# Attention with feature products feeding a gated unit: another plan for the order of the work, an fp32 down projection in the first slots, phi from PSUM, and later kv sums

## The chip, the cores and the metric

The kernel runs on one core of a Trainium2 chip. A core has engines that work side by side, each through its own instructions in order: TensorE (PE in the profile, its weight loads PEld), VectorE (DVE), ScalarE (ACT), GpSimd (POOL) and SyncE (SP), from whose queue all transfers here are issued. The metric is the device time of one execution in microseconds (us). Matmuls write to PSUM, everything else lives in SBUF; one tensor, called the scratch, lies in DRAM.

## The reference

A linear attention without softmax, and behind it a gated feed-forward layer. For 4 batches, 4 heads, 1088 positions and head size 32:

```
phi(x)[i*8+j] = (S1 x)[i] * (S2 x)[j]          # 8 x 8 = 64 features per head
kv  = sum over s of phi(k_s) v_s^T              # 64 x 32, per batch and head
z   = sum over s of phi(k_s)                    # 64
x   = phi(q) kv / (phi(q) z + 1e-6)             # 4352 rows of 128 (heads side by side)
xn  = x / sqrt(mean(x^2) + 1e-6) * rms_g
out = (silu(xn w_gate) * (xn w_val)) w_out      # 128 -> 1536 -> 128
```

Everything is float32. S1, S2 and the three weight matrices come as 64-bit words and are turned into float32 on VectorE (with one step that ScalarE can take).

## The kernel before, in words

**Chunks and slots.** The 4352 rows are cut into eight chunks of 512 and one of 256 columns. The 1536 hidden units are cut into twelve blocks j of 128. One *slot* is one chunk with one block: two products (gate into `g_ps`, value into `v_ps`, L682), a Silu on ScalarE (L689), the product `h` on VectorE (L693, one operand from PSUM, one from SBUF), and the down projection into `o_ps` (L713). Each of these products is made of three passes in a reduced-precision format, since each operand is split into a high and a low half: `h_hi` is a cast (L210, mostly ScalarE), `h_lo` the difference (L218 on VectorE or L217 on GpSimd). There are 108 slots. The first 24 run as blocks 0 to 5 for chunk 0, 0 to 5 for chunk 1, then 6 to 11 for each; later chunks run all twelve blocks. The last two slots (`EXACT`) take the down projection in one fp32 matmul (L700) with `w_end`, the sum of the two weight halves made on GpSimd (L748).

**Weights.** `weights(j)` loads one block of all three matrices (128 x 384 words), converts it in five steps on VectorE (L265 or, on ScalarE, L289; L269, L274, L279, L283), casts the high half (L210) and subtracts for the low half (L217/L218), each as one instruction over 384 columns.

**The kv side** (`kside`). For each batch: products with S1 and S2 (L425) into PSUM, a copy to SBUF by ScalarE (L440), the outer product phi (L431, GpSimd; for batch 0 VectorE may take it), then the sums. For batches 0 and 1 the matmuls of L459 sum kv and z at once. For batches in `TURNED` (2 and 3) the matmuls of L356 sum the transposed kv, GpSimd adds phi over the positions (`zsum`, four adds, L364), and a transpose (L378) and small matmuls (L383) bring both into place.

**The query side** (`qside`). Chunks 0 and 1 make phi in row layout: products (L492), a copy (L515), the outer product `phn` (L499, GpSimd or VectorE), transposes (L509), a copy (L527). Later chunks write the products (L538, L542) to the scratch (`far`, L544) and load them back repeated, two `at` (L548) and four `bt` (L555) loads for a chunk, and multiply (L561, GpSimd or VectorE). Then comes the numerator and denominator in one set of matmuls (L580), the division (L598, L599, L590), the mean square and its root (GpSimd, L625), scaling (L628), a transpose (L632) and the halves `x_hi` (L647) and `x_lo` (L635).

**What sets the order.** Every operation is a task with an estimated duration on each engine that may take it, a key, and the tiles that it reads and writes. `Plan.run` walks through an estimated time with one clock for an engine; among the tasks that are ready it takes the one with the smallest key. A slot's key is its number; side work has keys some slots before its due slot. Buffers of one name are taken in the order in which the tasks were added. The result fixes the order of each engine's instructions and of the transfers in SP's queue; on the chip an instruction starts when its data are there, and nothing else ties the engines together.

Of the kernel before, what the change touches and what calls it, by code (L numbers as in the profile page):

```python
# [20 lines left out]
R = 8  # L21
F = R * R
# [16 lines left out]
RAWS, WBUFS, TBUFS = 7, 3, 2  # L39
ACCUM = 2  # L40
MEAN = 0
LOOK = 350
# [3 lines left out]
PHI_DVE = 300  # L46
# [7 lines left out]
URGENT = -45  # L54
# [4 lines left out]
ABS_ACT = 150  # L59
# [5 lines left out]
TURNED = (2, 3)  # L65
HBUFS = 3
GAIN = -28.5
EXACT = 2
HEAD = 2
K1 = (14, 16, 18, -9)  # L70
K1O = ()
KVO = ()
Q0 = (-58, -50, -50)
Q0L = -97.8
Q1 = (9, 7, 6)
Q1L = -20
KO = -12
# [22 lines left out]
class Plan:  # L100
# [11 lines left out]
    def add(self, ways, key, reads=(), writes=()):  # L112
        deps = {self.writer[x] for x in reads}
# [35 lines left out]
    def run(self, clock, filler, slow, urgent, window):  # L149
        clock, todo, out = dict(clock), self.tasks, []  # L150
        while todo:
            found = {e: [] for e in clock}
            for t in todo[:window]:
                r = self.ready(t)
                if r is None:
                    continue
                e = min(t.ways, key=lambda e: max(clock[e], r) + t.ways[e][0] + t.ways[e][2])
                found[e].append((r, t))
# [5 lines left out]
            ns, emit, _ = t.ways[e]  # L164
# [13 lines left out]
def attention_then_glu(ctx, tc, kT, v, qT, sw, w, gain, out):  # L178
# [16 lines left out]
    def act(n, key, emit, reads, writes, sbuf=False):  # L195
        plan.add({"act": (n * 0.835 + (92 if sbuf else 51), emit, 0)}, key, reads, writes)

    def dve(ns, key, emit, reads, writes):
        plan.add({"dve": (ns + 68, emit, 0)}, key, reads, writes)
# [7 lines left out]
    def copy(n, key, out, in_, reads, writes, penalty=COPY_DVE):  # L207

        plan.add({
            "act": (n * 0.835 + 92, lambda: nc.scalar.copy(out=out(), in_=in_()), 0),  # L210
            "dve": (n * 0.52 + 68, lambda: nc.vector.tensor_copy(out=out(), in_=in_()), penalty),
        }, key, reads, writes)

    def rest(n, key, out, in_, hi, reads, writes, penalty=REST_DVE):
# [3 lines left out]
            "dve": (n * 1.04 + 68, lambda: nc.vector.tensor_tensor(out=out(), in0=in_(), in1=hi(), op=ALU.subtract), penalty),  # L218
# [26 lines left out]
    w_end = const.tile([P, max(EXACT, 1), P], F32, name="w_end")  # L245
# [13 lines left out]
    def to_f32(n, key, dst, raw, tmp, reads, tt, writes, side=None):  # L259
# [30 lines left out]

        plan.add({"dve": (n * 0.52 + 68, a, 0), "act": (n * 0.835 + 92, a_act, ABS_ACT)}, key, reads, tt)
        dve(n * 0.52, key, b, tt, tt)
        if side:
# [19 lines left out]
            dve(n * 0.52, key - 1, top, reads, apart)  # L313
            dve(n * 1.04, key - 1, low, [*reads, *apart], apart)
            dve(n * 0.52, key, shift, tt, tt)
            dve(n * 1.04, key, join, [*tt, *apart], writes)
            return
        dve(n * 0.52, key, c, tt, tt)
        dve(n * 1.04, key, e, (*reads, *tt), tt)
        dve(n * 1.04, key, f, (*reads, *tt), writes)  # L320
# [10 lines left out]

    def weights(j, key, early):
        raw = sb("w_raw", [P, 3 * P, 2], RAWS, U32)
        f, tmp = sb("w", [P, 3 * P], WBUFS), sb("w_tmp", [P, 3 * P], TBUFS)
# [6 lines left out]
        to_f32(3 * P, key, f, raw, tmp, [raw], [tmp], [f])  # L341
        hi, lo = (x[:, j].rearrange("p a n -> p (a n)") for x in (w_hi, w_lo))
        copy(3 * P, key, lambda: hi, f, [f], [("w_hi", j)])
        rest(3 * P, key, lambda: lo, f, lambda: hi.bitcast(F32), [f, ("w_hi", j)], [("w_lo", j)])
# [54 lines left out]
    def kside(b, keys, early):  # L399
# [15 lines left out]
        for i, (lo, hi) in enumerate(groups):  # L415
# [13 lines left out]
            def outer(eng, ab=ab, phi=phi, ts=ts, m=m):  # L429
                a = ab()[:, ts].rearrange("p t h c r -> p (t h) c r")  # L430
# [8 lines left out]
            act(
                HALF * m, kab, lambda ab=ab, ab_ps=ab_ps, ts=ts, m=m: nc.scalar.copy(  # L440
                    out=ab()[:, ts].rearrange("p t h c r -> p (t h) c r"),
                    in_=ab_ps()[:, :m * HALF].rearrange("p (th c r) -> p th c r", c=2, r=R),
                ), [ab_ps], [(ab, i)],
            )
# [30 lines left out]
    def qside(c, keys, early):  # L475
# [6 lines left out]
        if c < NATURAL:  # L482

            ab, pn = sb("abq", [P, 4, H, 2, R], 1), sb("phn", [P, 4, H * F], 1)
            for u in range(0, nt, 2):
                us = slice(u, u + 2)
# [326 lines left out]
```

## Time and profile before

| | |
|---|---|
| median of three runs | 300.51 us (296.71 to 304.61) |
| the profiled execution | 299.74 us |
| its span, from the first to the last instruction | 297.9 us |
| granted TensorE clock, mean | 0.971 |
| busy: PE, DVE, ACT, POOL | 275.7, 206.1, 157.2, 88.5 us |

The profile is one execution, seen by the hardware profiler. Busy times add the instructions of an engine; matmuls are pipelined and their ends are modelled, so that a busy TensorE need not be at its peak. "Idle before, releaser" tells how long an engine stood idle ahead of an instruction and what ended that. The chain of waits is followed back from the last instruction, at each step to what released it. The granted clock is the share of full speed that TensorE was given.

### The profile page before, as it was taken

How to read it: one execution, taken by the hardware profiler on the slowest of the kernel's cores; microseconds unless marked ns; L12 is line 12 of the kernel's file. 1: busy time of each engine (PE TensorE's matmuls, PEld its weight loads, DVE VectorE, ACT ScalarE, POOL GpSimd, SP SyncE). 2: the span in 40 equal slices, each digit the busy share in tenths (PEclk: the TensorE clock that was granted, in tenths of full speed). 3: DMA queues.
4: the chain of work that ended last, by engine and by line, in shares of the span. 5: the costliest groups of instructions: out<-in, count | busy, mean ns of one | idle time of the engine just before them, and what ended most of it. 6: DMA issues, size and time to landing. Idle time of an engine off the chain costs nothing.

```text
span 297.9 us, 4938 instructions
## 1 busy us (share of the span) xinstructions
PE 275.7 (93%) x1832; PEld 215.4 (72%) x1832; DVE 206.1 (69%) x370; ACT 157.2 (53%) x316; POOL 88.5 (30%) x82
## 2 busy tenths in 40 slices
PE   7886995897979999899699999999999999999995
PEld 5765773665757767678578677877786888788895
DVE  3799899997558656574765577468656966677531
ACT  4454563545535644365356366546645755565562
POOL 3165655447233392330310211103010302100062
PEclk9997796899999999999899999999999999999999
DMA  6975822000420005114104200411050102100000
GB/s 204 380 274 176 261 67 84 2 0 2 132 61 35 2 31 155 47 34 137 62 2 140 54 35 5 136 38 37 18 139 3 37 11 68 37 1 0 2 35 19
DMA packets 12680, 22.09 MB, mean 74 GB/s; under 512 B 1584, under 2 KB 5616, under 8 KB 12656
## 3 DMA queue, kind: packets, MB, share of 16 engines
q1 hardware_dynamic: 12656, 21.78, 23.2%
q8 instruction: 14, 0.23, 0.3%
q14 instruction: 10, 0.08, 0.1%
HBM read 18.69 MB, written 3.08 MB: 73 GB/s over the span
## 4 chain that ended last, share of the span: by engine, by line
PE 55%; DVE 14%; DMA 13%; SPq 5%; issue 4%; ACT 4%; POOL 4%; DVEq 0%; POOLq 0%; ACTq 0%
PE g_ps L682 16%; PE v_ps L682 15%; PE o_ps L713 15%; DMA bt<-far 8%; DMA far<-abt 3%; SPq L555 3%; PE att L580 3%; DVE h L693 3%; DVE w_tmp L279 2%; DVE w_tmp L269 2%; DVE h_lo L218 2%; SPq L548 2%; ACT h_hi L210 2%; DMA q<-qT 2%; PE att L538 1%
## 5 line engine op out<-in xcount | busy, mean ns | idle before, releaser
L210 ACT CAST h_hi<-h 128x512 fp32r<-128x512 f32 (+1 forms) x106 | 63.5, 600 | 89.0 <-DVE h L693 85.8
L218 DVE TENSOR_TENSOR h_lo<-h,h_hi 128x512 fp32r<-128x512 f32 x76 | 57.5, 757 | 40.0 <-ACT h_hi L210 39.6
L693 DVE TENSOR_TENSOR h<-v_ps,s 128x512 f32<-128x512 f32 (+2 forms) x109 | 70.9, 652 | 19.3 <-PE v_ps L682 11.6
L217 POOL TENSOR_TENSOR h_lo<-h,h_hi 128x512 fp32r<-128x512 f32 (+1 forms) x30 | 34.4, 1151 | 123.6 <-ACT h_hi L210 123.5
L689 ACT ACTIVATE s<-g_ps 128x512 f32<-128x512 f32 (+1 forms) x108 | 61.6, 571 | 11.3 <-PE g_ps L682 10.3
L682 PE MATMUL g_ps<-x_hi,w_hi 128*128 128x512 f32 (+2 forms) x111 | 45.8, 412 | 0.0
L682 PE MATMUL g_ps<-x_hi,w_lo 128*128 128x512 f32 (+2 forms) x111 | 42.6, 384 | 2.6 <-DVE w_lo L218 2.6
L682 PE MATMUL v_ps<-x_hi,w_hi 128*128 128x512 f32 (+2 forms) x111 | 43.7, 394 | 0.9 <-DVE h L693 0.9
L713 PE MATMUL o_ps<-h_lo,w_hi 128*128 128x512 f32 (+1 forms) x106 | 41.9, 395 | 2.0 <-POOL h_lo L217 1.0
L682 PE MATMUL g_ps<-x_lo,w_hi 128*128 128x512 f32 (+2 forms) x111 | 42.6, 384 | 0.0
L713 PE MATMUL o_ps<-h_hi,w_hi 128*128 128x512 f32 (+1 forms) x106 | 42.5, 401 | 0.0
L682 PE MATMUL v_ps<-x_hi,w_lo 128*128 128x512 f32 (+2 forms) x111 | 42.3, 381 | 0.0
L682 PE MATMUL v_ps<-x_lo,w_hi 128*128 128x512 f32 (+2 forms) x111 | 42.2, 380 | 0.0
L713 PE MATMUL o_ps<-h_hi,w_lo 128*128 128x512 f32 (+1 forms) x106 | 41.2, 389 | 0.0
L713 PEld LDWEIGHTS o_ps<-h_lo,w_hi 128*128 128x128 f32 x106 | 20.2, 191 | 9.2 <-DVE h_lo L218 3.1
L682 PEld LDWEIGHTS g_ps<-x_hi,w_lo 128*128 128x128 f32 x111 | 21.4, 192 | 7.5 <-DVE w_lo L218 2.9
L682 PEld LDWEIGHTS v_ps<-x_hi,w_hi 128*128 128x128 f32 x111 | 21.3, 192 | 6.4 <-DVE h L693 2.2
L682 PEld LDWEIGHTS g_ps<-x_hi,w_hi 128*128 128x128 f32 x111 | 21.2, 191 | 5.4 <-issue 1.0
L682 PEld LDWEIGHTS g_ps<-x_lo,w_hi 128*128 128x128 f32 x111 | 21.3, 192 | 4.5 <-DVE x_lo L635 0.2
L682 PEld LDWEIGHTS v_ps<-x_lo,w_hi 128*128 128x128 f32 x111 | 21.2, 191 | 4.3
L682 PEld LDWEIGHTS v_ps<-x_hi,w_lo 128*128 128x128 f32 x111 | 21.2, 191 | 4.0 <-issue 0.2
L713 PEld LDWEIGHTS o_ps<-h_hi,w_hi 128*128 128x128 f32 x106 | 20.1, 190 | 4.9 <-issue 0.4
(99 smaller groups left out, 307.4 us busy)
## 6 DMA issues: line engine op xcount, KB each, us to landing
w_raw<-w SPq DMA_DIRECT2D x12, 384.0 KB
at<-far SPq DMA_DIRECT2D x12, 256.0 KB
bt<-far SPq DMA_DIRECT2D x24, 128.0 KB
vt<-v SPq DMA_DIRECT2D x12, 204.0 KB
kt<-kT SPq DMA_DIRECT2D x12, 192.0 KB
q<-qT SPq DMA_DIRECT2D x8, 256.0 KB
outT<-o_sb SPq DMA_DIRECT2D x8, 256.0 KB
far<-abt SPq DMA_DIRECT2D x6, 128.0 KB
```

Source lines behind the costliest of these rows:

```text
L210: "act": (n * 0.835 + 92, lambda: nc.scalar.copy(out=out(), in_=in_()), 0),
L217: "pool": (n * 2.1 + 150, lambda: nc.gpsimd.tensor_tensor(out=out(), in0=in_(), in1=hi(), op=ALU.subtract), 0),
L218: "dve": (n * 1.04 + 68, lambda: nc.vector.tensor_tensor(out=out(), in0=in_(), in1=hi(), op=ALU.subtract), penalty),
L269: nc.vector.tensor_scalar(out=t, in0=t, scalar1=LEAST, scalar2=MOST, op0=ALU.max, op1=ALU.min)
L279: nc.vector.scalar_tensor_tensor(out=u, in0=r[:, :, 1], scalar=0xC0000000, in1=u, op0=ALU.bitwise_and, op1=ALU.bitwise_or)
L548: P * n * 4, kab, lambda p=p, rows=rows: nc.sync.dma_start(out=at()[:, p, :n], in_=far()[rows, :n].unsqueeze(1).to_broadcast([2 * R, R, n] ...
L555: F * n * 4, kab, lambda p=p, o=o, rows=rows: nc.sync.dma_start(out=bt()[o * F:(o + 1) * F, p, :n], in_=far()[rows, :n].unsqueeze(0).to_br ...
L580: nc.tensor.matmul(out=nv[hf * HALF:(hf + 1) * HALF, t, p, :], lhsT=phi()[:, p, l0:l0 + HALF], rhs=kvs[(s0 + l0) // S][:, p, :], start=Tru ...
L682: nc.tensor.matmul(out=acc()[:, cs], lhsT=wt[:, j, i3, :], rhs=x()[:, cs], start=(i == 0), stop=(i == 2))
L689: act(n, t + 0.3, lambda: nc.scalar.activation(out=s()[:, :n], in_=gps()[:, :n], func=AF.Silu), cols(gps, whole[0]), [s])
L693: lambda cs=cs: nc.vector.tensor_tensor(out=h()[:, cs], in0=vps()[:, cs], in1=s()[:, cs], op=ALU.mult),
L713: nc.tensor.matmul(out=o_ps()[:, :n], lhsT=wt[:, j, 2, :], rhs=x()[:, :n], start=first and i == 0, stop=last and i == 2,)
```

## The change

1. **The plan.** Each way of doing a task now carries a mark whether it uses the SBUF port that VectorE and GpSimd share (all of GpSimd's, and VectorE's with SBUF operands alone). `run` keeps one more clock, `port`: a marked task starts after the last marked one has ended, and where the other engine has a marked task with a smaller key, due before this one would end, that goes first. Fixed costs are raised (ScalarE 92 and 51 to 172 and 144 ns, VectorE 68 to 140), phi on GpSimd costs 530 ns a tile in place of 477, a step to a task of an engine that could take both costs 30 ns. The loads from the scratch count twice their bytes. `LOOK` goes from 350 to 150, `URGENT` from -45 to -1, `ABS_ACT` from 150 to -300.
2. **The first twelve slots** (`EARLY`) take the down projection as one fp32 matmul from `h` and `w_f`, the converted weights, which now stay in SBUF whole; `w_end` and its two GpSimd adds go. The high and low halves of the weights are made in two pieces, gate and value (256 columns) with the conversion, and w_out (128 columns) by tasks with keys from 6 to 16.
3. **Phi from PSUM.** For batch 0 (all groups but one), batch 1 and chunks 0 and 1 of the queries VectorE makes phi with the first factor straight from PSUM; ScalarE copies only the second factor. What is not made so goes to GpSimd.
4. **The kv side.** Batch 1 is turned as well. Batches 2 and 3, whose keys stood 12 slots before chunks 2 and 3, now stand 20, 18 and 16 slots before the chunks that first need them, 4 and 6. Batch 1's keys go from 14, 16, 18 to 8, 9, 10, and its tasks are added behind chunk 1's.
5. **Chunk 0's second half** of the query side has keys 20 later than the first.

The core of the diff:

```diff
-LOOK = 350
+LOOK = 150
-URGENT = -45
+URGENT = -1
-ABS_ACT = 150
+ABS_ACT = -300
-TURNED = (2, 3)
+TURNED = (1, 2, 3)
+EARLY = 12
+SPLIT = 6
-K1 = (14, 16, 18, -9)
+K1 = (8, 9, 10, -9)
-KO = -12
+KO = (20, 18, 16)
...
-            at = max(at, self.ready(t))
+            o = {"dve": "pool", "pool": "dve"}.get(e)
+            if o and t.ways[e][3]:
+                due = max(at, self.ready(t), port) + t.ways[e][0]
+                rivals = [x for r, x in found[o] if x.ways[o][3] and x.key < t.key and max(r, clock[o]) < due]
+                if rivals:
+                    e, t = o, min(rivals, key=lambda t: t.key)
+                    at = clock[o]
+            at = max(at, self.ready(t), port if t.ways[e][3] else 0)
...
+            if shared:
+                port = clock[e]
...
+    def split(j, xs, key):
+        n = (xs.stop - xs.start) * P
+        f, hi, lo = (x[:, j, xs].rearrange("p a n -> p (a n)") for x in (w_f, w_hi, w_lo))
+        ids = [(j, x) for x in range(xs.start, xs.stop)]
+        copy(n, key, lambda: hi, lambda: f, [("w", j)], [("w_hi", *y) for y in ids])
+        rest(n, key, lambda: lo, lambda: f, lambda: hi.bitcast(F32), [("w", j)] + [("w_hi", *y) for y in ids], [("w_lo", *y) for y in ids])
...
-        copy(3 * P, key, lambda: hi, f, [f], [("w_hi", j)])
-        rest(3 * P, key, lambda: lo, f, lambda: hi.bitcast(F32), [f, ("w_hi", j)], [("w_lo", j)])
+        split(j, slice(0, 2), key)
...
-            ways = {"pool": (m * 477, lambda outer=outer: outer(nc.gpsimd), 0)}
-            if first:
-                ways["dve"] = (m * 268 + 68, lambda outer=outer: outer(nc.vector), PHI_DVE)
-            plan.add(ways, kphi, [(ab, i)], [(phi, i)])
+            if near:
+                dve(m * 268, kphi, lambda outer=outer: outer(nc.vector), [(ab, i), ab_ps], [(phi, i)])
+            else:
+                pool(m * 530, kphi, lambda outer=outer: outer(nc.gpsimd), [(ab, i)], [(phi, i)])
...
-                    P * n * 4, kab, lambda p=p, rows=rows: nc.sync.dma_start(
+                    P * n * 8, kab, lambda p=p, rows=rows: nc.sync.dma_start(
...
-        if left < EXACT:
+        if left < EXACT or t < EARLY:
...
-                        out=o_ps()[:, cs], lhsT=w_end[:, left], rhs=h()[:, cs], start=first, stop=last and cs.stop == n
+                        out=o_ps()[:, cs], lhsT=w_f[:, j, 2], rhs=h()[:, cs], start=first, stop=last and cs.stop == n
...
-    kside(1, K1[:3], K1[3])
+    for j in range(NJ):
+        split(j, slice(2, 3), max(EARLY, slots.index((0, j))) + j % CUT - SPLIT if (0, j) in slots else 0)
     t1 = begin[1]
     qside(1, [t1 - x for x in Q1], Q1L)
+    kside(1, K1[:3], K1[3])
     for t, (c, j) in enumerate(slots):
         slot(c, j, t)
         if j == (CUT - 1 if c == 0 else NJ - 1):
-            if c + 2 < B:
-                kside(c + 2, [begin[min(len(begin) - 1, c + 2)] + KO] * 3, begin[c + 1] - 5)
             if c + 2 < len(CHUNKS):
                 t2 = begin[c + 2]
+                if c in (2, 4):
+                    kside(c // 2 + 1, [t2 - x for x in KO], t2 - KO[0] - 5)
                 qside(c + 2, [t2 - x for x in QO], t2 - 20)
```

More of the change, by code (lines that the diff above doesn't have):

```diff
@@ L149, in run @@
     def run(self, clock, filler, slow, urgent, window):
-        clock, todo, out = dict(clock), self.tasks, []
+        clock, todo, out, port = dict(clock), self.tasks, [], 0
         while todo:
@@ L195, in act, with dve @@
     def act(n, key, emit, reads, writes, sbuf=False):
-        plan.add({"act": (n * 0.835 + (92 if sbuf else 51), emit, 0)}, key, reads, writes)
-    def dve(ns, key, emit, reads, writes):
-        plan.add({"dve": (ns + 68, emit, 0)}, key, reads, writes)
+        plan.add({"act": (n * 0.835 + (172 if sbuf else 144), emit, 0)}, key, reads, writes)
+    def dve(ns, key, emit, reads, writes, shared=False):
+        plan.add({"dve": (ns + 140, emit, 0, shared)}, key, reads, writes)
     def pool(ns, key, emit, reads, writes):
@@ L289, in a_act @@
             nc.scalar.activation(out=t, in_=r[:, :, 1].bitcast(F32), func=AF.Abs)
-        plan.add({"dve": (n * 0.52 + 68, a, 0), "act": (n * 0.835 + 92, a_act, ABS_ACT)}, key, reads, tt)
-        dve(n * 0.52, key, b, tt, tt)
+        plan.add({"dve": (n * 0.52 + 140, a, 0, True), "act": (n * 0.835 + 172, a_act, ABS_ACT)}, key, reads, tt)
+        dve(n * 0.52, key, b, tt, tt, True)
         if side:
@@ L311, in join @@
                 )
[L313 to L316, printed above, removed]
+            dve(n * 0.52, key - 1, top, reads, apart, True)
+            dve(n * 1.04, key - 1, low, [*reads, *apart], apart, True)
+            dve(n * 0.52, key, shift, tt, tt, True)
+            dve(n * 1.04, key, join, [*tt, *apart], writes, True)
             return
-        dve(n * 0.52, key, c, tt, tt)
-        dve(n * 1.04, key, e, (*reads, *tt), tt)
-        dve(n * 1.04, key, f, (*reads, *tt), writes)
+        dve(n * 0.52, key, c, tt, tt, True)
+        dve(n * 1.04, key, e, (*reads, *tt), tt, True)
+        dve(n * 1.04, key, f, (*reads, *tt), writes, True)
     load(P * NB * 8, -99, lambda: nc.sync.dma_start(out=s_raw.rearrange("p n c -> p (n c)"), in_=sw.bitcast(U32)), ["s_raw"])
@@ L427, in mm, with outer @@
                         )
-            def outer(eng, ab=ab, phi=phi, ts=ts, m=m):
-                a = ab()[:, ts].rearrange("p t h c r -> p (t h) c r")
+            near = i not in FAR if first else b in NEAR
+            def outer(eng, ab=ab, phi=phi, ts=ts, m=m, near=near, ab_ps=ab_ps):
+                both = ab()[:, ts].rearrange("p t h c r -> p (t h) c r")
+                a = ab_ps()[:, :m * HALF].rearrange("p (th c r) -> p th c r", c=2, r=R) if near else both
                 eng.tensor_tensor(
@@ L482, in qside @@
         if c < NATURAL:
-            ab, pn = sb("abq", [P, 4, H, 2, R], 1), sb("phn", [P, 4, H * F], 1)
+            ab, pn = sb("abq", [P, 4, H, R], 1), sb("phn", [P, 4, H * F], 1)
             for u in range(0, nt, 2):
+                kab = keys[0] + (LATER if first and u else 0)
                 us = slice(u, u + 2)
@@ L571, in qside @@
         for u in range(0, nt, 2):
+            knum = keys[1] + (LATER if first and u else 0)
             num, den, rden, sq = ps("att", 3), sb("den", [P, 8, 1], 2), sb("rden", [P, 8, 1], 2), sb("sq", [P, 2, DM], 2)
@@ L612, in qside @@
                 267, knum, lambda u=u, sq=sq: nc.vector.tensor_reduce(out=ss()[:, u:u + 2], in_=sq(), axis=AX.X, op=ALU.add),
-                [sq], [(ss, u), (ss, u + 1)],
+                [sq], [(ss, u), (ss, u + 1)], True,
             )
         for u, wd in ((0, 2), (2, 2)) if first else ((0, nt),):
+            kturn = keys[2] + (LATER if first and u else 0)
             us, cs = slice(u, u + wd), slice(u * P, (u + wd) * P)
@@ L716, in down @@
                     )
-            pe(n * 1.36, t + 2.5, down, [h_hi, h_lo, ("w_hi", j), ("w_lo", j)], cols(o_ps, whole[0]))
+            pe(n * 1.36, t + 2.5, down, [h_hi, h_lo, ("w_hi", j, 2), ("w_lo", j, 2)], cols(o_ps, whole[0]))
         if not last:
```

94 lines of the change are left out of this document (43 added, 51 removed).

## The prediction

> **What bounds the kernel now.** I read the page first, then a cut of the span into stages, the chain of waits, the groups of instructions, and last the instructions in order of time where these pointed. On the page TensorE is busy nearly always and the chain is mostly TensorE; that is an average over stages that differ, so the cut comes next (columns: length of the stretch, busy time of each engine with its count, granted clock, DMA).
>
> ```profile
> PE 275.7 (93%) x1832; PEld 215.4 (72%) x1832; DVE 206.1 (69%) x370; ACT 157.2 (53%) x316; POOL 88.5 (30%) x82
> ```
> ```profile
> 20.00:66.00 46.00, 39.38 (x290) 29.42 (x288) 44.95 (x74) 23.16 (x54) 26.04 (x18) 0.85 0.35 112
> 66.00:85.00 19.00, 16.98 (x152) 12.60 (x151) 13.20 (x19) 10.30 (x20) 7.89 (x8) 1.00 0.28 73
> 85.00:169.00 84.00, 77.38 (x502) 59.06 (x500) 52.21 (x92) 41.52 (x75) 27.81 (x21) 0.98 0.21 63
> 169.00:293.00 124.00, 123.41 (x672) 99.99 (x673) 82.46 (x150) 72.15 (x139) 20.30 (x22) 1.00 0.12 36
> ```
>
> From 169 to 293 us TensorE is busy 123.4 of 124 us: nothing but fewer matmuls can shorten that stage. From 20 to 66 us VectorE is busy 44.95 of 46 us and the granted clock is down to 0.85: VectorE is the bound there. From 85 to 169 us TensorE lacks 6.6 us. The gain has to come from the front and the middle.
>
> Why VectorE is full in front is seen in single instructions (start, duration, engine).
>
> ```profile
> 28.04 0.35 DVE L269 TENSOR_SCALAR w_tmp<-w_tmp 128x384 f32<-128x384 f32 x1
> 28.31 0.55 DVE L279 SCALAR_TENSOR_TENSOR w_tmp<-w_raw,w_tmp 128x384 uint32<-128x384 uint32 x1
> 28.78 0.35 DVE L274 TENSOR_SCALAR w_tmp<-w_tmp 128x384 uint32<-128x384 uint32 x1
> 29.05 0.55 DVE L283 SCALAR_TENSOR_TENSOR w<-w_raw,w_tmp 128x384 uint32<-128x384 uint32 x1
> ...
> 21.87 1.66 DVE L274 TENSOR_SCALAR w_tmp<-w_tmp 128x384 uint32<-128x384 uint32 x1
> 23.72 1.85 DVE L279 SCALAR_TENSOR_TENSOR w_tmp<-w_raw,w_tmp 128x384 uint32<-128x384 uint32 x1
> ...
> 104.44 0.69 DVE L693 TENSOR_TENSOR h<-v_ps,s 128x512 f32<-128x512 f32 x1 [1.19 <-PE v_ps L682]
> ```
> ```profile
> 21.51 1.81 POOL L431 TENSOR_TENSOR phi<-ab 128x768 f32<-128x768 f32 x1 [0.71 <-ACT ab L440]
> 23.60 1.56 POOL L431 TENSOR_TENSOR phi<-ab 128x768 f32<-128x768 f32 x1 [0.28 <-ACT ab L440]
> ...
> 102.67 5.35 POOL L431 TENSOR_TENSOR phi<-ab 128x768 f32<-128x768 f32 x3
> ```
>
> The steps of a weight conversion take 0.35 and 0.55 us; the two that start just after a GpSimd phi take 1.66 and 1.85 and end when it has ended. The h product at 104.44, which reads PSUM and one SBUF tile, takes its usual 0.69 in the middle of GpSimd's phis. So SBUF work of the two engines excludes each other, and an operand from PSUM escapes it. The groups give the bill.
>
> ```profile
> L279 DVE SCALAR_TENSOR_TENSOR w_tmp<-w_raw,w_tmp 128x384 uint32<-128x384 uint32 x12 | 11.0, 916 | 0.0
> L283 DVE SCALAR_TENSOR_TENSOR w<-w_raw,w_tmp 128x384 uint32<-128x384 uint32 x12 | 9.8, 814 | 0.0
> L269 DVE TENSOR_SCALAR w_tmp<-w_tmp 128x384 f32<-128x384 f32 x12 | 7.6, 637 | 0.0
> L274 DVE TENSOR_SCALAR w_tmp<-w_tmp 128x384 uint32<-128x384 uint32 x12 | 6.6, 550 | 0.1
> L431 POOL TENSOR_TENSOR phi<-ab 128x768 f32<-128x768 f32 x10 | 18.1, 1817 | 7.9 <-ACT ab L440 7.9
> L431 DVE TENSOR_TENSOR phi<-ab 128x768 f32<-128x768 f32 x1 | 1.0, 959 | 0.0
> L217 POOL TENSOR_TENSOR h_lo<-h,h_hi 128x512 fp32r<-128x512 f32 x20 | 27.1, 1358 | 100.4 <-ACT h_hi L210 100.3
> L364 POOL TENSOR_TENSOR zsum<-phi 128x768 f32<-128x768 f32 x2 | 3.7, 1836 | 0.1
> ```
>
> Against 0.55 and 0.35 us, the four conversion steps lose 12 x (0.37 + 0.26 + 0.29 + 0.20) = 13.4 us to waiting, nearly all of it between 20 and 66 us. VectorE's own work there is then 45 - 13 = 32 us, beside 26 us of GpSimd.
>
> **The change, part by part. The front.** Of GpSimd's 26.0 us go: the three phi of batch 1 (to VectorE, from PSUM), 3 x 1.8 = 5.5; two phi and a first zsum add of batch 2 (later), 5.5; about seven h_lo, as the twelve first slots go down whole in fp32, 7 x 1.36 = 9.5; one query phi, 1. That is 21.5. New there: batch 1 is turned now and has zsum adds, two of 1.84 and two shorter ones, 5.5 us in all by an estimate of half length for the short; and the low halves of the weights, now in two pieces a weight (24 instead of 12, the second pieces around slots 6 to 16). Where these land is the plan's choice: none on GpSimd or all of them, 0 to about 13 us (twelve of 0.75 and twelve of 0.35, scaled from the phi rate by length); I take 4. GpSimd keeps 4.5 + 5.5 + 4 = 14 us, and with waiting in proportion VectorE loses 13 x 14/26 = 7 us instead of 13. Bounds: 2 us, if its adds fall beside the products from PSUM, to 13, if they don't.
>
> VectorE's own work stays about equal: three h_lo less and the mask step moved to ScalarE for most weights (about -3), against three phi of 0.96 and one more query phi (+3.8). Its new phi reads one operand from PSUM; the h product shows that as neither slower nor blocked. ScalarE has room: 23.2 of 46 us busy, with twelve h_hi casts gone and some conversions and twelve short copies added. Up to the end of the weights VectorE has 32 + 7 = 39 us in place of 45; counted on to 85 us it has 32 + 11 of its own (the 13.2 of the second row less some 2 of waiting) and 7 + 2 of waiting: 52 us where the stretch was 65 us long.
>
> TensorE's floor for the same slots, from the chain of waits in order of time (start, duration, what):
>
> ```profile
> 26.84 0.84 PE att L425 x12
> 27.68 1.23 PE att L459 x24
> 28.91 1.05 PE att L492 x4
> 36.35 0.71 PE g_ps L682 x3
> 67.66 0.81 PE att L356 x48
> 73.89 0.88 PE att L538 x2
> 75.39 2.58 DMA far<-abt
> 81.21 5.10 DMA bt<-far
> ```
>
> A slot is three such triples, 2.1 us; 17 of them to 85 us are 35.7. Beside them lie the 72 phi matmuls of batches 1 and 2 at 0.07 us (5.0), batch 1's 72 L459 (3.7), batch 2's 72 L356 (1.2), L538 (0.9) and about 5 of chunk 1's query side and the turning (an estimate from the 1.05 row): 51 us of 65. The change takes out batch 2 (36 L425, 72 L356 and its turning, 4 us in all, which come back later) and makes batch 1's 72 L459 into 72 L356 plus a turning (-2). The fp32 down is bounded by the L538 row, one fp32 matmul over 512 columns: 0.88 against 0.71, so twelve slots cost +2 us, and most of it lies under VectorE's bound. Floor: 51 - 4 - 2 + 2 = 47 us, below VectorE's 52. Add 2 for gaps between the two, and slot 17 stands at 20 + 54 = 74 instead of 85. With batch 2's 4 us repaid in a stage that TensorE bounds, the front is worth 11 - 4 = 7 us, from 0 (waits not reduced) to 14 (TensorE's floor).
>
> By the page on the gate ("TensorE: Matmul & The Clock Gate", What's actually happening) of the Trainium skill the clock halves after an idle window of about 3.4 us. Were the 0.85 of the front to stay, 47/0.85 = 55 us would be that floor, and the front would be worth 6. No run here shows yet whether the clock recovers when VectorE is relieved.
>
> **The middle.** TensorE's own waits between 85 and 169 us, and the clock after the longest:
>
> ```profile
> 87.84 1.04 PE L580 MATMUL att<-kv,phiq 128*64 128x66 f32 x28 [1.69 <-POOL phiq L561]
> 123.69 1.04 PE L580 MATMUL att<-kv,phiq 128*64 128x66 f32 x28 [1.42 <-DVE phiq L561]
> 145.13 1.04 PE L580 MATMUL att<-kv,phiq 128*64 128x66 f32 x28 [2.30 <-POOL phiq L561]
> 146.10 0.67 PE L713 MATMUL o_ps<-h_hi,w_hi 128*128 128x512 f32 x1
> 149.86 0.39 PE L713 MATMUL o_ps<-h_hi,w_hi 128*128 128x512 f32 x1
> ```
>
> All three are the numerator's matmuls, put into TensorE's order before phi is there. Phi waits for the scratch: 2.58 us for the store and, from its end at 77.97 to the end of the last load at 86.31, 8.3 us for six loads. The old plan believes in 0.77 us for an `at` load, 0.39 (raised to its least step of 0.5) for a `bt`, and 1.9 after the last: 5.4 us. The new doubles the loads: 2 x 1.54 + 4 x 0.77 + 1.9 = 8.1, which is what the trace has. The numerator and phi should then be placed where their data are. That returns 1.69 + 1.42 + 2.30 = 5.4 us, and the slow clock after the last wait another 1.7 (nine passes in 3.76 us instead of 2.1). What is late next is the same phi with batch 2's and 3's GpSimd work near it, so I take 5.4 and not 7.1. Lower bound: a loss of 3, two such waits in chunks that now have none.
>
> The moved kv work issues six loads for each batch on SP's queue, ahead of a later chunk's query and scratch loads. Its keys stand 20 slots, 42 us, before their chunk, so I price it at nothing; without that lead its 1.2 MB would be some 4 us more in front of a phi. The other edits (the plan's higher fixed costs, shorter look-ahead, key changes, the second half of chunk 0 later, no separate end weights) only choose the order; they carry no term of their own, and the ranges hold them.
>
> **Sum.** The profiled execution took 299.74 us, 1.84 over its span of 297.9. Span after: 297.9 - 7 - 5.4 = 285.5; with the 1.84, 287.3; it stood 0.8 below the median of the runs. I forecast 287.
>
> **The rivals.** *The order reserves nothing* (294 to 300 us, chance 0.20). The plan books VectorE and GpSimd as one, but no wait in the program keeps them apart; GpSimd starts when its data are there. If the zsum adds and low halves fill what the h_lo leave, VectorE still loses 11 of its 13 us, the front gives 2 less the 4 repaid, and the middle 5: 297.9 + 2 - 5 = 295 of span, 297. For it: 0 to 13 us of low halves are the plan's choice. Against: 21.5 us of GpSimd work really leave. Beside this stands a rule of the Trainium skill ("SBUF — State Buffer", Who interferes with whom): the shared port pair is an exclusive lock, whoever issues first keeps it for the whole instruction. The rows at 21.87 and 23.72 agree.
>
> *The moved kv work stalls the TensorE-bound stage* (slower; 306 and above, chance 0.13). Batches 2 and 3 now run their phi and zsum, 7 GpSimd instructions each, beside later slots.
>
> ```profile
> 110.21 2.06 DVE L218 TENSOR_TENSOR h_lo<-h,h_hi 128x512 fp32r<-128x512 f32 x1
> ```
> ```profile
> 113.74 0.40 PE L383 MATMUL att<-ones,zsum 128*64 128x2 f32 x8 [0.41 <-POOL zsum L364]
> ```
>
> Here an h_lo waited 1.4 us for a zsum, and the next h with it. With batch 1's four adds that is 18 such holds; at 1.4 us each on TensorE, 25 us are lost against 12.4 won: 297.9 + 12.6 + 1.8 = 312, and 306 if every fourth is hidden. It decides once h comes over a slot late, which two g and v buffers don't cover. Against it: batch 3 ran through exactly this from 102 to 114 us, and TensorE waited 0.41 us for its zsum.
>
> *TensorE's floor all through* (277 to 281, chance 0.15). Front 14, middle 7.1: 297.9 - 21.1 + 1.8 = 278.6. For it: VectorE's bound of 52 us is only 5 above the floor. Against: in-order engines leave gaps.
>
> **Chances and range.** The forecast's own case (281 to 293) has 0.52. A measurement here can tell about 2% from no change, so 294.5 and 306.5 are the borders. Faster: 0.52 + 0.15 and 0.02 of the first rival, 0.69; within: its other 0.18; slower: 0.13. The range reaches from the floor's 277 to the first rival's 300, leaving out the slower case and little more.
>
> **What would show it.** In the profile after: the four conversion steps at means well below 0.9, 0.8, 0.6 and 0.55 us; VectorE's full stretch ending near 60; the clock between 20 and 66 us above 0.85; slot 17 near 74; no L580 matmul waiting over 1 us for phiq; the last 125 us unchanged but for the kv pieces. Wrong it would be if GpSimd's time before 66 us stays near 26 us, or if TensorE waits for zsum or for h in the stage after 100 us.

## The result and the profile after

The changed kernel takes 277.44 us in the median of four runs (275.39 to 279.52); the kernel before, run beside it, 300.26 us. The ratio is 0.9277, with a 95% interval of 0.915 to 0.9403: faster by 7.2%. Medians are over all executions of a kernel, while the ratios leave out executions more than 1.5% above its fastest. The forecast was 287 us, faster, in a range of 277 to 300. The direction was right, the gain some 1.7 times what was forecast, and the time lies only 0.4 us inside the range, where the third rival, TensorE's floor all through, had put it.

The profiled execution took 276.29 us with a span of 274.5. The page's busy times and its chain, as answers to the page shown before:

```profile
PE 264.6 (96%) x1835; PEld 206.8 (75%) x1835; DVE 186.4 (68%) x348; ACT 153.4 (56%) x316; POOL 102.9 (37%) x107
...
PE 81%; DMA 8%; SPq 3%; DVE 3%; POOL 2%; ACT 1%; issue 1%; POOLq 0%; DVEq 0%
```

The cut into the stages of the prediction (same columns: length, busy time and count of PE, PEld, DVE, ACT and POOL, granted clock, DMA share, GB/s):

```profile
20.00:66.00 46.00, 45.09 (x344) 31.46 (x342) 38.99 (x78) 27.86 (x72) 24.26 (x30) 1.00 0.42 136
66.00:85.00 19.00, 19.00 (x83) 15.10 (x83) 13.63 (x23) 10.97 (x20) 3.94 (x4) 1.00 0.30 77
85.00:169.00 84.00, 82.43 (x631) 64.07 (x630) 54.53 (x92) 45.45 (x84) 44.51 (x34) 1.00 0.16 50
169.00:270.50 101.50, 101.50 (x566) 83.71 (x566) 66.60 (x120) 59.34 (x112) 25.26 (x26) 1.00 0.13 40
```

TensorE is now busy 45.1 of the 46 us from 20 to 66 where it was 39.4, and its clock stands at 1.00 where it was 0.85. VectorE has 7 us free in that stretch. The column to look at twice is the fifth: GpSimd still works 24.3 us there (26.0 before). The middle stage lacks 1.6 us of TensorE instead of 6.6.

How far the slots had come is read from the h products in order of time. These are those of slots 17 and 47, before:

```profile
84.59 0.69 DVE L693 TENSOR_TENSOR h<-v_ps,s 128x512 f32<-128x512 f32 x1
...
171.34 0.68 DVE L693 TENSOR_TENSOR h<-v_ps,s 128x512 f32<-128x512 f32 x1
```

and after:

```profile
68.16 0.68 DVE L718 TENSOR_TENSOR h<-v_ps,s 128x512 f32<-128x512 f32 x1
...
142.99 0.69 DVE L718 TENSOR_TENSOR h<-v_ps,s 128x512 f32<-128x512 f32 x1 [0.58 <-PE v_ps L707]
```

By its h, slot 17 is 16.4 us earlier, the stretch from there to slot 47 takes 74.8 us where it took 86.8, 11.9 us less, and the rest 4.9 us more. An h is an instruction of VectorE, though, and can stand behind other work there. How far TensorE had come shows in the last matmul of the value product of the same two slots, before:

```profile
84.10 0.39 PE L682 MATMUL v_ps<-x_lo,w_hi 128*128 128x512 f32 x1
...
167.68 0.39 PE L682 MATMUL v_ps<-x_lo,w_hi 128*128 128x512 f32 x1
```

and after:

```profile
67.04 0.39 PE L707 MATMUL v_ps<-x_lo,w_hi 128*128 128x512 f32 x1
...
142.49 0.39 PE L707 MATMUL v_ps<-x_lo,w_hi 128*128 128x512 f32 x1
```

By TensorE, slot 17 is 17.1 us earlier, the stretch to slot 47 is 8.1 us shorter (75.5 instead of 83.6), with one kv batch inside it in both kernels, and the rest is 1.8 us longer, as batch 3 of the kv side now lies there: 17.1 + 8.1 - 1.8 = 23.4, the difference of the spans. The h of slot 47 came 0.1 us after its product in the kernel after, and 3.3 us after it in the kernel before, where two phi products of a later chunk stood ahead of it in VectorE's order and waited for the scratch:

```profile
165.59 0.69 DVE L561 TENSOR_TENSOR phiq<-at,bt 128x512 f32<-128x512 f32 x1 [3.00 <-DMA bt<-far]
...
167.68 1.77 DVE L561 TENSOR_TENSOR phiq<-at,bt 128x512 f32<-128x512 f32 x1 [0.79 <-DMA bt<-far]
```

The groups of the weights' work, as answer to the bill of the prediction (partitions x elements, count, busy us, mean ns, idle before and releaser):

```profile
L298 DVE SCALAR_TENSOR_TENSOR w_f<-w_raw,w_tmp 128x384 uint32<-128x384 uint32 x12 | 7.7, 646 | 0.1
L294 DVE SCALAR_TENSOR_TENSOR w_tmp<-w_raw,w_tmp 128x384 uint32<-128x384 uint32 x12 | 7.6, 646 | 0.1
L284 DVE TENSOR_SCALAR w_tmp<-w_tmp 128x384 f32<-128x384 f32 x12 | 5.5, 466 | 1.7 <-ACT w_tmp L304 1.7
L289 DVE TENSOR_SCALAR w_tmp<-w_tmp 128x384 uint32<-128x384 uint32 x12 | 5.2, 448 | 0.1
...
L232 POOL TENSOR_TENSOR w_lo<-w_f,w_hi 128x256 fp32r<-128x256 f32 x12 | 9.0, 751 | 19.3 <-ACT w_hi L225 19.3
L232 POOL TENSOR_TENSOR w_lo<-w_f,w_hi 128x128 fp32r<-128x128 f32 x12 | 6.7, 559 | 8.2 <-ACT w_hi L225 8.2
```

By the prediction's reckoning (0.55 and 0.35 us unhindered) the four steps now wait 12 x (0.096 + 0.096 + 0.116 + 0.098) = 4.9 us, against 13.4. All 24 low halves of the weights went to GpSimd, 15.7 us, more than the highest value the prediction had allowed.

TensorE's numerators and the other waits in the middle (start, duration, then in brackets the idle time and what ended it):

```profile
88.15 0.50 PE L738 MATMUL o_ps<-h_lo,w_hi 128*128 128x512 f32 x1 [1.49 <-POOL h_lo L232]
89.98 1.16 PE L604 MATMUL att<-kv,phiq 128*64 128x66 f32 x32
113.21 0.40 PE L403 MATMUL att<-ones,zsum 128*64 128x2 f32 x8
122.11 1.16 PE L604 MATMUL att<-kv,phiq 128*64 128x66 f32 x32
```

The numerators (L604) come in one piece with no wait, and so do the small matmuls that need zsum. What is left is one wait for an h_lo on GpSimd.

### The profile page after: what moved, and what is told of

Read it like the earlier page. It is cut to its first block, busy times and chain, and to the rows that moved or that the text cites. A ratio compares the mean times of both kernels' runs of the same rounds, so it can differ in the third digit from the quotient of the medians.

```text
span 274.5 us, 4960 instructions
## 1 busy us (share of the span) xinstructions
PE 264.6 (96%) x1835; PEld 206.8 (75%) x1835; DVE 186.4 (68%) x348; ACT 153.4 (56%) x316; POOL 102.9 (37%) x107
## 4 chain that ended last, share of the span: by engine, by line
PE 81%; DMA 8%; SPq 3%; DVE 3%; POOL 2%; ACT 1%; issue 1%; POOLq 0%; DVEq 0%
PE g_ps L707 24%; PE v_ps L707 23%; PE o_ps L738 21%; DMA bt<-far 4%; PE att L604 3%; PE o_ps L725 3%; DMA far<-abt 3%; DMA w_raw<-w 2%; PE att L561 2%; PE att L445 1%; PE att L657 1%; SPq L578 1%; PE att L376 1%; DVE h_lo L233 1%; SPq L571 1%
## 5 line engine op out<-in xcount | busy, mean ns | idle before, releaser
L225 ACT CAST h_hi<-h 128x512 fp32r<-128x512 f32 (+1 forms) x88 | 52.4, 595 | 53.1 <-DVE h L718 51.9
L233 DVE TENSOR_TENSOR h_lo<-h,h_hi 128x512 fp32r<-128x512 f32 x64 | 49.9, 782 | 23.4 <-ACT h_hi L225 22.5
L232 POOL TENSOR_TENSOR h_lo<-h,h_hi 128x512 fp32r<-128x512 f32 (+1 forms) x30 | 32.9, 1103 | 56.2 <-ACT h_hi L225 52.5
L707 PE MATMUL g_ps<-x_hi,w_hi 128*128 128x512 f32 (+2 forms) x111 | 47.1, 424 | 0.0
L707 PE MATMUL g_ps<-x_lo,w_hi 128*128 128x512 f32 (+2 forms) x111 | 41.8, 377 | 0.0
L738 PE MATMUL o_ps<-h_lo,w_hi 128*128 128x512 f32 (+1 forms) x94 | 36.2, 385 | 1.6 <-POOL h_lo L232 1.5
L584 POOL TENSOR_TENSOR phiq<-at,bt 128x512 f32<-128x512 f32 (+1 forms) x14 | 18.2, 1302 | 50.6 <-DMA bt<-far 50.6
L738 PE MATMUL o_ps<-h_hi,w_hi 128*128 128x512 f32 (+1 forms) x94 | 36.9, 392 | 0.0
L738 PE MATMUL o_ps<-h_hi,w_lo 128*128 128x512 f32 (+1 forms) x94 | 35.9, 382 | 0.0
L232 POOL TENSOR_TENSOR w_lo<-w_f,w_hi 128x256 fp32r<-128x256 f32 (+1 forms) x24 | 15.4, 655 | 27.6 <-ACT w_hi L225 27.5
```

Of the source, the lines that this page charges most:

```text
L225: "act": (n * 0.835 + 172, lambda: nc.scalar.copy(out=out(), in_=in_()), 0),
L232: "pool": (n * 2.1 + 150, lambda: nc.gpsimd.tensor_tensor(out=out(), in0=in_(), in1=hi(), op=ALU.subtract), 0),
L233: "dve": (n * 1.04 + 140, lambda: nc.vector.tensor_tensor(out=out(), in0=in_(), in1=hi(), op=ALU.subtract), penalty, True),
L584: eng.tensor_tensor(out=phi()[:, p, :n], in0=at()[:, p, :n], in1=bt()[:, p, :n], op=ALU.mult)
L707: nc.tensor.matmul(out=acc()[:, cs], lhsT=wt[:, j, i3, :], rhs=x()[:, cs], start=(i == 0), stop=(i == 2))
L738: nc.tensor.matmul(out=o_ps()[:, :n], lhsT=wt[:, j, 2, :], rhs=x()[:, :n], start=first and i == 0, stop=last and i == 2,)
```

## The experiments

Two theories were to be told apart for each part: that the part removes a wait which nothing else removes, or that it only reorders work beside a bound that stands elsewhere. The first four kernels undo one part of the changed kernel each; the next three do one part alone on the kernel before; then follow the later kv undone, parts together, and two variants of the changed kernel. Each ratio is to the kernel before, run on the same chip beside it. Start times of slots are those of the profiled execution and, where nothing else is said, of the h.

**No booking of the port.**

```diff
-        ways = {e: (*w, e == "pool")[:4] if len(w) < 4 else w for e, w in ways.items()}
+        ways = {e: (*w[:3], False) for e, w in ways.items()}
```

> The changed kernel, with the plan's booking of the shared port taken out (no task is marked, so the port's clock and the right of way between VectorE and GpSimd fall away); operations, estimates and keys stay. Theory A (the gain is work that left the two engines, the booking itself reserves nothing on the chip): 276 to 281 us, VectorE's conversion steps at means below 0.75 us for the two long ones. Theory B (the gain is the order that the booking makes): the front fills up again, 285 to 295 us, long steps at 0.8 us or more, TensorE short of work between 20 and 60 us.

Measured: 278.55 us, ratio 0.9337 (0.9283 to 0.9391), not to be told from the changed kernel's 0.9277 (0.915 to 0.9403). The long conversion steps:

```profile
L298 DVE SCALAR_TENSOR_TENSOR w_f<-w_raw,w_tmp 128x384 uint32<-128x384 uint32 x12 | 7.2, 599 | 0.1
L294 DVE SCALAR_TENSOR_TENSOR w_tmp<-w_raw,w_tmp 128x384 uint32<-128x384 uint32 x12 | 7.1, 593 | 0.1
```

Without the booking the steps wait no longer than with it. Theory A holds, as far as the two intervals can tell: the clock and right of way that the plan gained are not what the time came from. The prediction's first rival was right in that the order reserves nothing, and wrong in that the gain would fail for it.

**The scratch at its old estimate.**

```diff
-                    P * n * 8, kab, lambda p=p, rows=rows: nc.sync.dma_start(
+                    P * n * 4, kab, lambda p=p, rows=rows: nc.sync.dma_start(
...
-                        F * n * 8, kab, lambda p=p, o=o, rows=rows: nc.sync.dma_start(
+                        F * n * 4, kab, lambda p=p, o=o, rows=rows: nc.sync.dma_start(
```

> The changed kernel, with the loads from the scratch estimated at their bytes as before (0.77 and 0.39 us in place of 1.54 and 0.77). Theory A (the estimate gave the middle its gain): TensorE waits again for phi in three or more chunks, 1.4 to 2.3 us each, with the half clock after the longest: 282 to 287 us. Theory B (those waits went because other work around them changed): 276 to 279 us and no TensorE wait for phi over 1 us.

Measured: 290.38 us, ratio 0.9706 (0.9636 to 0.9777): 13 us of the 23 are gone, more than either theory said. The instructions of its L604 that waited:

```profile
62.80 1.04 PE L604 MATMUL att<-kv,phiq 128*64 128x66 f32 x28 [2.03 <-POOL phiq L584]
...
90.88 1.04 PE L604 MATMUL att<-kv,phiq 128*64 128x66 f32 x28 [1.99 <-POOL phiq L584]
...
126.57 1.81 PE L604 MATMUL att<-kv,phiq 128*64 128x66 f32 x28 [2.13 <-POOL phiq L584]
...
191.71 0.57 PE L604 MATMUL att<-kv,phiq 128*64 128x66 f32 x12 [1.89 <-POOL phiq L584]
```

With two shorter ones they are 10.1 us, in four chunks. The one at 126.57 runs its 28 matmuls in 1.81 us where 1.04 is usual: the clock was down. Four chunks wait here, three did in the kernel before. Slot 17 is at 70.2 us, 2.0 later than in the changed kernel, slot 47 at 154.1, 11.1 later.

**No fp32 down in the first slots.**

```diff
-EARLY = 12
+EARLY = 0
```

> The changed kernel, with no slot but the last two going down in fp32 (EARLY 0), so that twelve h_hi casts and twelve h_lo come back to the front and TensorE saves 12 x 0.16 = 2 us. Theory A (the fp32 down is a large part of what relieved VectorE): VectorE is full again between 20 and 60 us, 281 to 287 us. Theory B (phi from PSUM and the later kv are enough, TensorE is the bound with room to spare): 275 to 278 us.

Measured: 286.45 us, ratio 0.9609 (0.9537 to 0.9682). Theory A's time; its sign was not quite there. VectorE was busy 34.2 us of the 40 between 20 and 60 us, no more than in the changed kernel. The loss comes behind: slot 11 is 3.3 us late and slot 17 10.3. In that stretch of TensorE and of VectorE:

```profile
64.25 0.34 PE L604 MATMUL att<-kv,phiq 128*64 128x66 f32 x4 [1.88 <-POOL phiq L584]
66.06 1.04 PE L604 MATMUL att<-kv,phiq 128*64 128x66 f32 x28 [1.47 <-POOL phiq L584]
```
```profile
66.68 0.17 DVE L622 TENSOR_SCALAR den<-att 128x8 f32<-128x8 f32 x1 [3.63 <-PE att L604]
```

TensorE waits for chunk 2's phi, VectorE stands 3.63 us behind the numerator that waits, and the weights still to be converted (slots 12 to 17 need six of them) stand behind that. That the h_lo which came back to GpSimd are what made phi late there is argued from this order, not shown by a run.

**Phi of batches 0 and 1 on GpSimd.**

```diff
-FAR = (1,)
-NEAR = (1,)
+FAR = (0, 1, 2, 3)
+NEAR = ()
```

> The changed kernel, with the phi of batches 0 and 1 made on GpSimd from SBUF (FAR all groups, NEAR none). Theory A (phi through the shared port blocks VectorE): 4.5 us of GpSimd phi for batch 1 come back into the front and the first slot starts 1 to 2 us later: 280 to 285 us. Theory B (VectorE's own time counts, and is relieved of 2.9 us): 275 to 278 us.

Measured: 280.61 us, ratio 0.935 (0.9261 to 0.9439), which overlaps the changed kernel's interval. The median lies in theory A's range, but by the intervals it is undecided: phi from PSUM is worth 2 to 3 us by the ratios and medians, and may be worth nothing. One thing its profile does show. GpSimd is busy 26.6 us between 20 and 66 us here, as much as in the kernel before, with batch 1's three phi at 1.6 us each back on it, and still the four conversion steps stand at 762, 689, 389 and 370 ns: 4.9 us of waiting, as in the changed kernel.

**The fp32 down alone on the kernel before** (`w_end` and its adds go, and the converted weights stay in `w_f`).

```diff
-        if left < EXACT:
+        if left < EXACT or t < EARLY:
...
-                        out=o_ps()[:, cs], lhsT=w_end[:, left], rhs=h()[:, cs], start=first, stop=last and cs.stop == n
+                        out=o_ps()[:, cs], lhsT=w_f[:, j, 2], rhs=h()[:, cs], start=first, stop=last and cs.stop == n
```

> The kernel before, with the first twelve slots' down projection in one fp32 matmul from whole weights kept in SBUF (the end weights' two GpSimd adds go as well), all estimates and keys as before. Theory A (work that leaves VectorE and GpSimd in front is time): 9.5 us of GpSimd h_lo and 2 of VectorE's go between 20 and 66 us, TensorE pays at most 2: 291 to 296 us. Theory B (one part alone leaves the waits where they are): 298 to 303 us.

Measured: 299.16 us, ratio 0.9952 (0.9899 to 1.0005): 0 to 3 us. Theory B by the median. The profiled execution is the shortest of the ten, 295.73 us, its span 3.9 us below that of the kernel before. In it slot 11's h stands at 64.2 instead of 68.9 us, and slot 17's at 83.9 instead of 84.6. What held the latter, on VectorE:

```profile
80.86 0.69 DVE L563 TENSOR_TENSOR phiq<-at,bt 128x512 f32<-128x512 f32 x1 [3.52 <-DMA bt<-far]
81.46 0.68 DVE L695 TENSOR_TENSOR h<-v_ps,s 128x512 f32<-128x512 f32 x1
```

Chunk 2's phi had been put before the h's in VectorE's order and waited 3.52 us for the scratch. TensorE did not lose the gain there, however: with the value product of slot 17 it is 3.8 us ahead of the kernel before, with that of slot 24 3.2:

```profile
80.33 0.39 PE L684 MATMUL v_ps<-x_lo,w_hi 128*128 128x512 f32 x1
```

So this trace shows the scratch in the way of VectorE, and not that it took the gain back, as the expectation of the kernel with three parts, further down, has it. Why most of the other executions keep so little is open.

**The scratch's estimate alone.**

```diff
-                    P * n * 4, kab, lambda p=p, rows=rows: nc.sync.dma_start(
+                    P * n * 8, kab, lambda p=p, rows=rows: nc.sync.dma_start(
...
-                        F * n * 4, kab, lambda p=p, o=o, rows=rows: nc.sync.dma_start(
+                        F * n * 8, kab, lambda p=p, o=o, rows=rows: nc.sync.dma_start(
```

> The kernel before, with only the loads from the scratch estimated at twice their bytes. Theory A: TensorE's waits of 1.69, 1.42 and 2.30 us for phi go, with the half clock after the last: 292 to 296 us. Theory B (the waits belong to the crowded front and move with it): 298 to 303 us.

Measured: 291.44 us, ratio 0.9725 (0.9639 to 0.9811). Theory A: no numerator of a chunk behind the second waits for its phi any more. By TensorE's value products slot 17 is 1.2 us later than before (85.30), slot 47 5.7 us earlier (161.97), and the span 8.0 shorter: most of the gain lies in the middle.

**The later kv alone.**

```diff
-            if c + 2 < B:
-                kside(c + 2, [begin[min(len(begin) - 1, c + 2)] + KO] * 3, begin[c + 1] - 5)
...
+                if c in (2, 4):
+                    kside(c // 2 + 1, [t2 - x for x in KO], t2 - KO[0] - 5)
```

> The kernel before, with only batches 2 and 3 of the kv side moved to 20, 18 and 16 slots before chunks 4 and 6. Theory A: 5.5 us of GpSimd leave the stretch of 20 to 66 us, but 4 us of TensorE work are paid back later: 296 to 300 us, about no change. Theory B (the moved work stalls the stage that TensorE bounds): 303 us or more. Theory C (it is a main part of the gain): below 294 us.

Measured: 293.38 us, ratio 0.9705 (0.9566 to 0.9844). Theory C by the median, and more than the forecast gave it: 6 us by the medians, 9 by the ratio. Its profile is of an execution with a late start, so no slot times are taken from it. Of its waits of TensorE, these concern the numerators and the moved sums (waiting instruction, what ended the wait, us in total, times, longest):

```profile
PE att L383 <- POOL zsum L364: 1.3, 2, 0.7
...
PE att L580 <- POOL phiq L561: 0.6, 1, 0.6
```

The kernel before waits 4.0 and 1.4 us for phi in the same view, so the later kv removes mostly the same waits as the estimate does: with batches 2 and 3 elsewhere, the store of chunk 2 to the scratch is issued at 55.2 us instead of 75.4, that of chunk 3 at 85.7 instead of 111.8. The prediction's slower rival, stalls for zsum in the stage that TensorE bounds, is 1.3 us here, and the waits for an h_lo are 3.7 us in all instead of 1.9.

**The early kv in the changed kernel.**

```diff
-                if c in (2, 4):
-                    kside(c // 2 + 1, [t2 - x for x in KO], t2 - KO[0] - 5)
+            if c + 2 < B:
+                kside(c + 2, [begin[c + 2] - 12] * 3, begin[c + 1] - 5)
```

> The changed kernel, with batches 2 and 3 of the kv side at their old places (12 slots before chunks 2 and 3, batch 2 added ahead of chunk 2's query side). Theory A: batch 2's 9 to 10 us of GpSimd come back into the front, where VectorE had 5.5 us free of 40, and chunk 2's query side waits for it: 280 to 285 us. Theory B (the front has room now): 275 to 279 us.

Measured: 282.21 us, ratio 0.9397 (0.9306 to 0.9487), some 5 us over the changed kernel's median; the two intervals overlap by a little (0.9306 to 0.9403). Theory A by its time, and by its waits. Its stretch of 60 to 85 us, and three waits of TensorE there:

```profile
60.00:85.00 25.00, 21.38 (x175) 15.63 (x173) 16.10 (x27) 10.49 (x22) 16.03 (x14) 0.86 0.21 59
```
```profile
66.33 0.33 PE L398 MATMUL att<-ident,kv_both 128*128 128x128 f32 x1 [0.39 <-ACT kv_both L391]
68.88 0.40 PE L403 MATMUL att<-ones,zsum 128*64 128x2 f32 x8 [1.35 <-POOL zsum L384]
72.50 0.79 PE L738 MATMUL o_ps<-h_lo,w_hi 128*128 128x512 f32 x1 [1.88 <-DVE h_lo L233]
```

GpSimd is busy 16.0 us of 25 (9.9 in the changed kernel over the same stretch), the sums and an h_lo hold TensorE, and the clock drops to 0.86.

**Scratch and kv together on the kernel before**, and **both with the fp32 down**. The edits are those shown above for the single parts.

> The kernel before, with both the doubled estimate for the scratch and batches 2 and 3 later; alone they gave 291.4 and 293.4 us. Theory A (both remove the same waits for phi in the middle): not the sum, 288 to 291 us. Theory B (they act in different places): the sum of 8 and 6, 284 to 287 us.

> The same with the fp32 down in the first twelve slots as well, which alone gave nothing (299.2 us) since the 4.7 us that it had won by slot 11 were lost again by slot 17, where phi of chunk 2 waited for the scratch. Theory A (a gain in front is kept only when the next wait is gone): 4 us or more below the kernel with the other two, 280 to 286 us. Theory B (the fp32 down is worth nothing without phi from PSUM and the new costs): within 2 us of it.

Measured: 287.88 us, ratio 0.9614 (0.954 to 0.9687), for two, and 282.69 us, 0.9462 (0.9413 to 0.9512), for three. The product of the two single ratios would be 0.944, with an interval of about 0.928 to 0.960 worked out from theirs, which still meets that of the two together. That they remove in part the same waits is read from the waits for phi, which either part alone removes almost whole, and fits theory A's time. The fp32 down, worth 0 to 3 us alone, is worth 5 us on top of them. The four conversion steps, 35.0 us in the kernel before, take 32.6 us with two parts and 26.7 with three; one of them, with two and with three:

```profile
L283 DVE SCALAR_TENSOR_TENSOR w<-w_raw,w_tmp 128x384 uint32<-128x384 uint32 x12 | 8.8, 732 | 0.0
```
```profile
L284 DVE SCALAR_TENSOR_TENSOR w_f<-w_raw,w_tmp 128x384 uint32<-128x384 uint32 x12 | 6.6, 546 | 0.0
```

Three parts account for 16 of some 22 us (both ratios taken from the 298.0 us of that comparison). The rest (0.9462 against 0.9277, intervals just apart) lies among phi from PSUM, batch 1 turned, the weights in two pieces, the mask step on ScalarE, the keys and the booking. Removing phi from PSUM or the booking alone can't be told from nothing; taking back the fixed costs lost nothing; the others were not tried one by one; which of them carries it stays open.

**Six fp32 slots instead of twelve.**

```diff
-EARLY = 12
+EARLY = 6
```

> The changed kernel, with the fp32 down in six slots instead of twelve: TensorE saves 1 us, six h_lo and six h_hi come back. With none it was 286.5, with twelve 277.4 us. Theory A (all of the relief is needed): half way, 280 to 284 us. Theory B (the first six are the narrow place): 275 to 278 us, better than both kernels by up to 1 us.

Measured: 283.83 us, ratio 0.949 (0.9421 to 0.956). In theory A's range, by the ratios nearer to no such slot (0.9609) than to twelve (0.9277). The first h is at 25.4 us (23.2 with twelve), slot 5 at 38.4 (36.2), slot 11 at 54.5 (52.6), slot 17 at 76.3 (68.2): behind the late start, the loss lies between slots 11 and 17. Between 60 and 85 us:

```profile
64.22 0.80 PE L707 MATMUL g_ps<-x_hi,w_lo 128*128 128x512 f32 x1 [3.02 <-POOL w_lo L232]
```

A low half of weights came 3 us late from GpSimd, and half the clock followed. Slots 6 to 11 run while the second six weights are made; that these lacked the relief is argued from this order.

**The old fixed costs in the changed kernel.**

```diff
-        plan.add({"act": (n * 0.835 + (172 if sbuf else 144), emit, 0)}, key, reads, writes)
+        plan.add({"act": (n * 0.835 + (92 if sbuf else 51), emit, 0)}, key, reads, writes)
...
-        plan.add({"dve": (ns + 140, emit, 0, shared)}, key, reads, writes)
+        plan.add({"dve": (ns + 68, emit, 0, shared)}, key, reads, writes)
...
-            at = max(at, d.end + (0 if d.on == "pe" and "pe" in t.ways else 30 if d.on in t.ways else self.HOP))
+            at = max(at, d.end + (0 if d.on == "pe" and "pe" in t.ways else self.HOP))
```

> The changed kernel, with the old fixed costs in the plan (ScalarE 92 and 51 ns, VectorE 68, no 30 ns step on the same engine), the scratch's doubled estimate kept. Theory A (they only choose the order and carry no term): 276 to 281 us. Theory B (a plan that runs ahead of the chip puts numerators too early again): 283 us or more, with TensorE waiting for phi.

Measured: 274.23 us (272.5 to 275.9), ratio 0.9184 (0.911 to 0.9259). It is not slower than the changed kernel, and its median is the lowest of all; the intervals overlap, so that it is faster isn't settled. Its TensorE waits 1.0 us in all for VectorE and 0.2 for a numerator's phi. The raised fixed costs show no gain of their own; the scratch's figure does.

## Why the prediction was right, and where it was not

**The bound.** That the late stage could give nothing, and that the gain had to come from the front and the middle, held: from slot 47 on TensorE needs 1.8 us more, with 3.4 us of batch 3's matmuls now there, where the prediction had put 4 for a kv batch. The fp32 down's price was not hidden under VectorE's bound as forecast, since TensorE became the bound: from 20 us to slot 17's h it is busy 47.3 of 48.2 us.

**The front: mis-sized, 11 us against 17.1 (16.4 by the h).** Two steps failed. The first is "GpSimd keeps 4.5 + 5.5 + 4 = 14 us, and with waiting in proportion VectorE loses 13 x 14/26 = 7 us instead of 13". GpSimd kept 24.3 us, since 22 pieces of the low halves, 13.9 us, went there where 4 had been taken, and by the prediction's own test ("Wrong it would be if GpSimd's time before 66 us stays near 26 us") the front should have stayed full. It did not: the steps' waiting fell to 4.9 us all the same. GpSimd's total was the wrong measure. What made the waiting fall stays open. The booking is excluded by the kernel without it (long steps at 593 and 599 ns), and phi from PSUM alone by the kernel with phi on GpSimd, which waits 4.9 us beside 26.6 us of GpSimd. The shorter pieces of low halves are not needed for it either: the kernel before with three parts makes them whole, and its steps wait 5.1 us, against 11.0 without the fp32 down.

The second is "VectorE's own work stays about equal". From 20 us to slot 17's h VectorE is busy 57.75 us before and 41.20 after, 16.55 less, which is the size of the front's gain. The four steps give 8.6 of it. The rest is work that left: h_lo 7.3 us (two in place of ten, where the prediction had three fewer), low halves of weights 5.6 (none in place of eight), mask steps 1.4; against that stand 2.8 us of batch 1's phi and some 2 us of other work (instructions overlap a little at their ends, so that these times add to 17.9). VectorE was no longer the bound, and slot 17 came at 68.2, beside the 67 of TensorE's floor and not the 74 of VectorE's bound with its gaps.

**The middle: mis-sized, 5.4 us against 8.1 of TensorE from slot 17 to 47.** The term taken was the three waits alone, 5.4; the 1.7 us of the slow clock, which the prediction had set aside for kv work that might get in the way, came as well, and so did 0.34 + 0.41 us of waits for batch 3's phi and zsum (the numerator's and the sums' waits are gone from the trace). Chunk 2's numerator, 1.2 us, moved in front of slot 17, and one new wait of 1.5 us for an h_lo goes off: 7.5 of the 8.1 us. The mechanism was shown both ways: the scratch's figure alone gives 8 us, and without it the changed kernel loses 13. The clock of 0.85 did not stay: by the row of 20 to 66 us it is 1.00 there once TensorE is fed, so it was a mark of the bound and not a bound. With the rule of the Trainium skill ("TensorE: Matmul & The Clock Gate", What's actually happening), that idle windows throttle and sustained work releases, this row agrees; the floor of 55 us that the prediction drew from a clock that stays did not apply.

That the time still fell inside the stated range is in part luck: both terms of the gain were too small, the price of the moved kv batch was too large, and 277.44 us is 0.4 us above the range's lower end.

**The parts do not add.** The prediction added a front and a middle. The runs show that they were linked: the fp32 down alone is worth 0 to 3 us, 5 us once scratch and kv are mended, and 9 us when it is taken from the finished kernel. The later kv, priced at 5.5 us of GpSimd less 4 of TensorE, gave 6 to 9 alone, with most of TensorE's waits for phi gone as chunk 2's and 3's query sides start earlier.

**The rivals.** "The order reserves nothing" was true of the booking and gave the wrong time. The slower one failed: batch 2's and 3's sums cost TensorE nothing in the changed kernel, though one hold of the kind it named is there, an h_lo of 2.37 us behind a zsum:

```profile
104.71 2.37 DVE L233 TENSOR_TENSOR h_lo<-h,h_hi 128x512 fp32r<-128x512 f32 x1
107.57 0.69 DVE L718 TENSOR_TENSOR h<-v_ps,s 128x512 f32<-128x512 f32 x1 [0.49 <-PE att L398]
```

The next h was not late for it: it waited for TensorE. TensorE's floor, at a chance of 0.15, gave 278.6, from 14 us in front and 7.1 in the middle, and is what happened (15.3 with the late stage's 1.8 taken off, and 8.1); the objection to it, that in-order engines leave gaps, was given too much weight.

## What to carry to other kernels

Where several engines run in a fixed order made from estimates, the one estimate that is far off (here a DRAM round trip taken for 5.4 us that lasts 8) can be worth more than many that are a little off: look in the trace for a first instruction of a group that waits each time for the same transfer. Judge a part by taking it out of the finished kernel as well as by adding it alone: here the same part gave 0 to 3 us one way and 9 the other. Read how far a kernel has come from the engine that bounds it, since an instruction of another engine may stand late for a reason of its own. For engines that exclude each other, look at the waits inside the instructions, and not at the other engine's total.

## What the runs showed of the hardware that was not expected

VectorE's waiting for GpSimd fell from 13.4 to 4.9 us while GpSimd's busy time in the same stretch went only from 26.0 to 24.3 us. GpSimd's busy time holds waiting as well: this phi of the kernel before takes 2.77 us where others of its shape take 1.56 and 1.81, while the four VectorE steps from 28.04 to 29.05 us run beside it at their usual 0.35 and 0.55 us.

```profile
28.19 2.77 POOL L431 TENSOR_TENSOR phi<-ab 128x768 f32<-128x768 f32 x1 [3.03 <-ACT ab L440]
```

The granted clock of 0.85 in the front came back to 1.00 with nothing done to the clock. And the start differs between profiled executions: in some the first transfers run slower, as in the kernel with the later kv alone,

```profile
0.00:20.00 20.00, 17.42 (x189) 13.50 (x190) 9.16 (x30) 7.54 (x24) 5.39 (x14) 0.74 0.74 249
```

against the kernel before, whose first transfers are issued in the same order,

```profile
0.00:20.00 20.00, 16.66 (x210) 12.62 (x211) 12.81 (x37) 9.31 (x28) 6.49 (x16) 1.00 0.81 282
```

with 249 GB/s against 282 and the first h at 30.1 against 26.7 us. Why is open; slot times of different profiles are comparable only with that in mind.
